# Row-tiled attention scores for two heads at once, with a 0/1 mask multiplied in on VectorE

## The chip, the cores and the metric

The kernel runs on one core of a Trainium2 chip. A core has five engines with instruction streams of their own: TensorE (PE) multiplies matrices, VectorE (DVE) and ScalarE (ACT) work element by element, GpSimd (POOL) does the same on data outside the matmul result memory PSUM, and SyncE (SP) issues DMA transfers. ACT and POOL issue transfers as well. Each engine takes its instructions in the order of the program and waits on semaphores that other engines raise. Weight loads of PE are shown apart as PEld; they run beside the matmuls. SBUF is the on-chip data memory, PSUM takes the matmul results.

The metric is the device time of one execution in microseconds; the median over the runs counts. The kernel before takes 332.96 us (three runs, 329.74 to 333.13).

## What is computed

Block-sparse attention (4 batches, 8 heads, 768 positions, head size 64), followed by a feed-forward layer with a squared relu. The mask consists of 32x32 blocks: neighbours, the first and last block row and column, and three sampled blocks per row.

```python
scores = scale * np.matmul(q, k.transpose(0, 1, 3, 2))
...
scores = np.where(mask, scores, -1000000000.0)
scores = scores - np.max(scores, axis=-1, keepdims=True)
attn = np.exp(scores)
attn = attn / (np.sum(attn, axis=-1, keepdims=True) + 1e-09)
return np.matmul(attn, v).astype(np.float32)
...
h = x @ w_in            # x: heads side by side, 3072 x 512; w_in 512 x 2048
r = np.maximum(h, 0.0)
g = r * r
return (g @ w_out).astype(np.float32)
```

## The kernel before

**Units.** Heads are taken in pairs. A pair of one batch is a unit `u` (16 of them, four per batch). The 768 queries are cut into three parts `qi` of 256, the 768 keys into six blocks of 128, taken two at a time as `cp` (three). One slot `(u, qi, cp)` is the score tile of two key blocks and two heads against 256 queries; there are 144. Batch 0 goes through its four pairs for `qi` = 0, then for 1 and 2; the later batches go unit by unit.

**A slot.** `scores` (L319) makes four matmuls of 256 columns into a PSUM tile `ps` (two buffers, L66). `exps` (L332) turns the tile into `pT` on ACT, one instruction of 128x1024 to bf16, seven buffers. `values` (L337) makes four matmuls into `po` (one buffer). `VA` and `VB` hold V of one head in one half and ones in the other, so `po` also holds the sums. After three slots `inverse` (L352) makes 1/sum with three ACT instructions (Ln, Ln, Exp), and `normalize` (L361) multiplies on DVE into `xT`.

**The mask before.** It costs no instruction of its own in a slot. Of the 128 rows that a matmul contracts over, 64 hold the head and 24 more hold the mask: in the keys a one-hot of the key's block (`oh`, L200), in the queries minus 8e9 where that block is not allowed (`bm`, `pb`, L232 to L241). So the contraction has 88 rows, and the product is already masked. The two heads lie in separate tiles `QK[i][:, which, h]`, 24 mask rows under each; they are copied there by DMA (`key_rows`, `query_rows`) or, from batch 1 on, come in through the transposing DMA from the tiles `CQ`, whose columns 64 to 87 hold the mask (`mask_columns`, L250).

**Preparing a unit.** Q, K and V of a pair are loaded as fp32 by three DMAs (`load`, L144). For batch 0, Q and K are cast on DVE, transposed on PE (`transp`, L274) and moved to `QK` on DVE, one copy per head (`evac`, L282). Later units are cast on DVE into `CQ` (`cast_t`, L287) and transposed by DMA, four per unit (`transp_dma`, L290). V is cast on POOL for the units 1 to 3 and on DVE for the others (L269).

**Feed-forward.** Nine tiles of 256 (batch 0) or 384 positions. `hidden` (L376): for each of 16 blocks of `w_in` four matmuls into `ph` (two buffers, shared with the transposes), relu on DVE (`relu`, L387), the square on POOL (`square`, L392). `output` (L400): 16 matmuls of 512 columns into `py` (one buffer), copied out by ACT (L411) and stored by SP. A tile needs all four pairs of its batch, so the feed-forward of a batch runs beside the attention of the next, and the rest at the end. The weights come through POOL's DMA queue, `w_in` first (L303).

**What sets the order.** Every step is a `Task` with an engine, an assumed duration, a priority and its dependencies (L79). `run_schedule` (L108) plays these through once at build time: the engine that can start first takes its ready task of lowest key. The order it comes to is the fixed instruction order of each engine. On the chip only the semaphores act; where a step takes longer than assumed, everything behind it on its engine waits. Attention has keys from 0 to 143 (relus 0), hidden and output from 1000 on, so PE takes attention work where it is ready, and feed-forward work otherwise.

The softmax here doesn't subtract the row's maximum and nothing guards it: scores larger than these inputs give would overflow.

## Time and profile before

One execution was taken by the hardware profiler. It took 334.34 us, of which 332.6 lie in the span of its records.

| | |
|---|---|
| median of three runs | 332.96 us |
| the profiled execution / its span | 334.34 us / 332.6 us |
| first exp / first hidden matmul | 11.5 us / 38.9 us |
| first hidden matmul of batch 1 | 140.4 us |
| last value matmul | 264.5 us |
| exp of a slot, 128x1024 (ACT, L334) | 144 of 1.017 us on average |
| the three instructions of `inverse` (ACT, L356 to L358) | 48 each, 0.381, 0.376 and 0.416 us |
| the two of `normalize` (DVE, L367, L368) | 48 each, 0.414 and 0.427 us |
| relu of 128x384 (DVE, L389), square (POOL, L395) | 96 each, 0.557 and 0.837 us |

Engines overlap, so busy times do not add up to the span. Matmuls are pipelined: the profile gives 0.27 us for one of 256 columns, but the next starts 0.109 us later. In the views that list instructions, a line has the start in us, the length, the engine, the line of the program, the operation, output <- input with their shapes, and in square brackets how long the engine had been idle and what ended that. In the grouped view a line has the count after the x, then busy us, mean ns of one, and the idle time before them with what ended it. PEclk is the share of its clock that PE was granted.

### The profile page before, as it was taken

How to read it: one execution, taken by the hardware profiler on the slowest of the kernel's cores; microseconds unless marked ns; L12 is line 12 of the kernel's file. 1: busy time of each engine (PE TensorE's matmuls, PEld its weight loads, DVE VectorE, ACT ScalarE, POOL GpSimd, SP SyncE). 2: the span in 40 equal slices, each digit the busy share in tenths (PEclk: the TensorE clock that was granted, in tenths of full speed). 3: DMA queues.
4: the chain of work that ended last, by engine and by line, in shares of the span. 5: the costliest groups of instructions: out<-in, count | busy, mean ns of one | idle time of the engine just before them, and what ended most of it. 6: DMA issues, size and time to landing. Idle time of an engine off the chain costs nothing. (4 is left out here: it accounts for less than half of the span.)

```text
span 332.6 us, 5743 instructions
## 1 busy us (share of the span) xinstructions
PE 306.5 (92%) x2174; PEld 209.8 (63%) x2174; DVE 156.6 (47%) x336; ACT 210.2 (63%) x317; POOL 129.3 (39%) x183
## 2 busy tenths in 40 slices
PE   2878899999978978999999999999999999999994
PEld 1555687777855756677776766777776655555541
DVE  7674244885454532366545334344334454444410
ACT  5479897859857778887786978888886301000011
POOL 6157143452422310055444232322223456666610
PEclk9999799999999999999999999999999999999999
DMA  7989995599999997482326200000000000100002
GB/s 228 233 195 206 199 289 211 120 250 229 216 285 239 246 271 225 95 204 42 62 67 73 55 2 32 2 32 3 32 33 1 34 33 32 63 34 32 34 32 96
DMA packets 59561, 39.61 MB, mean 119 GB/s; under 512 B 39790, under 2 KB 56462, under 8 KB 59534
## 3 DMA queue, kind: packets, MB, share of 16 engines
q1 hardware_dynamic: 55038, 34.66, 41.2%
q0 software_dynamic: 4224, 4.19, 7.8%
q10 hardware_dynamic: 272, 0.39, 0.3%
q8 instruction: 17, 0.28, 0.3%
q14 instruction: 10, 0.08, 0.1%
HBM read 27.26 MB, written 6.29 MB: 101 GB/s over the span
## 5 line engine op out<-in xcount | busy, mean ns | idle before, releaser
L395 POOL TENSOR_TENSOR g<-r 128x384 bf16<-128x384 f32 (+1 forms) x144 | 111.0, 776 | 175.7 <-DVE r L389 175.5
L334 ACT ACTIVATE pT<-ps 128x1024 bf16<-128x1024 f32 x144 | 140.9, 1017 | 41.2 <-PE po L349 32.0
L384 PE MATMUL ph<-xT,w_in_sb 128*128 128x384 bf16 (+1 forms) x576 | 120.0, 308 | 2.3 <-DVE r L389 2.1
L389 DVE TENSOR_SCALAR r<-ph 128x384 f32<-128x384 f32 (+1 forms) x144 | 73.1, 512 | 98.3 <-PE ph L384 72.8
L408 PE MATMUL py<-w_out_sb,g 128*128 128x512 bf16 x384 | 110.1, 379 | 0.8 <-ACT ys L413 0.8
L384 PEld LDWEIGHTS <-w_in_sb 128*128 128x128 bf16 x576 | 56.2, 98 | 38.2 <-issue 3.6
L347 PE MATMUL po<-pT,VA 128*128 128x256 bf16 x288 | 71.3, 274 | 7.7 <-DVE xT L368 4.6
L326 PE MATMUL ps<-QK 88*128 88x256 bf16 x288 | 72.6, 277 | 3.0 <-ACT pT L334 1.6
L328 PE MATMUL ps<-QK 88*128 88x256 bf16 x288 | 72.0, 276 | 0.4 <-DVE QK L285 0.2
L349 PE MATMUL po<-pT,VB 128*128 128x256 bf16 x288 | 71.1, 274 | 0.0
L413 ACT COPY ys<-py 128x512 f32<-128x512 f32 x24 | 13.9, 585 | 62.5 <-PE py L408 58.6
L408 PEld LDWEIGHTS <-g 128*128 128x128 bf16 x384 | 37.5, 98 | 22.0 <-issue 1.3
L347 PEld LDWEIGHTS <-VA 128*128 128x128 bf16 x288 | 28.2, 98 | 19.5 <-issue 8.6
L328 PEld LDWEIGHTS <-QK 88*128 88x128 bf16 x288 | 28.6, 99 | 10.4 <-issue 2.3
L326 PEld LDWEIGHTS <-QK 88*128 88x128 bf16 x288 | 28.2, 98 | 9.2 <-issue 1.9
L349 PEld LDWEIGHTS <-VB 128*128 128x128 bf16 x288 | 28.3, 98 | 8.7 <-issue 1.6
L367 DVE TENSOR_TENSOR xT<-po,rs 64x256 bf16<-64x256 f32 x48 | 19.9, 414 | 29.0 <-ACT rs L358 27.3
L356 ACT ACTIVATE ls<-po 64x256 f32<-64x256 f32 x48 | 18.3, 381 | 10.2 <-PE po L349 9.1
L358 ACT ACTIVATE rs<-ls 128x256 f32<-128x256 f32 x48 | 20.0, 416 | 1.5
L368 DVE TENSOR_TENSOR xT<-po,rs 64x256 bf16<-64x256 f32 x48 | 20.5, 427 | 0.6
L357 ACT ACTIVATE ls<-po 64x256 f32<-64x256 f32 x48 | 18.1, 376 | 0.6
L288 DVE CAST CQ<-ks 128x768 bf16<-128x768 f32 x12 | 6.9, 578 | 11.8 <-DMA QK<-CQ 11.7
(49 smaller groups left out, 76.2 us busy)
## 6 DMA issues: line engine op xcount, KB each, us to landing
qs<-in_q_dram SPq DMA_DIRECT2D x16, 384.0 KB, 6.2
vs<-in_v_dram SPq DMA_DIRECT2D x16, 384.0 KB, 8.1
out_dram<-ys SPq DMA_DIRECT2D x24, 256.0 KB, 2.1
ks<-in_k_dram SPq DMA_DIRECT2D x15, 384.0 KB, 8.7
w_in_sb<-in_moe_w_in_dram POOLq DMA_DIRECT2D x4, 512.0 KB, 8.2
w_out_sb<-in_moe_w_out_dram POOLq DMA_DIRECT2D x4, 512.0 KB, 13.4
QK<-CQ SPq DMA_TRANSPOSE x48, 4.0
ks<-in_k_dram ACTq DMA_DIRECT2D x1, 384.0 KB
```

Source lines behind the costliest of these rows:

```text
L326: nc.tensor.matmul(ps[:, c, 0, :], KA[i][0:64 + nb, ksl], QA[i][0:64 + nb, qsl], start=True, stop=True)
L328: nc.tensor.matmul(ps[:, c, 1, :], KB[i][0:64 + nb, ksl], QB[i][0:64 + nb, qsl], start=True, stop=True)
L334: nc.scalar.activation(out=pT, in_=stile.pop((u, qi, cp)), func=AF.Exp, scale=scale)
L347: nc.tensor.matmul(po[:, 0, :], VA[i][:, n, :], pT[:, c, 0, :], start=first, stop=last, skip_group_check=True)
L349: nc.tensor.matmul(po[:, 1, :], VB[i][:, n, :], pT[:, c, 1, :], start=False, stop=last, skip_group_check=True)
L358: nc.scalar.activation(out=rs, in_=ls, func=AF.Exp, scale=-1.0)
L367: V.tensor_mul(out=xT[b][0:D, a, qsl], in0=po[0:D, 0, :], in1=rs[0:D, :])
L368: V.tensor_mul(out=xT[b][D:P, a, qsl], in0=po[D:P, 1, :], in1=rs[D:P, :])
L384: nc.tensor.matmul(ph, w_in_sb[:, kc, f * P:(f + 1) * P], xT[b][:, kc, c0:c0 + w], start=(kc == 0), stop=(kc == KM - 1))
L389: V.tensor_scalar(out=r, in0=htile.pop((T, f)), scalar1=0.0, scalar2=None, op0=AOP.max)
L395: G.tensor_mul(out=g, in0=r, in1=r)
L408: nc.tensor.matmul(py, gtile[T, f][:, ts * P:(ts + 1) * P], w_out_sb[:, f, :], start=(f == 0), stop=(f == NF - 1))
```

## The change

**Row tiling.** Q and K of a pair now lie in one tile each, `QT` and `KT`, head 0 in the rows 0 to 63 and head 1 in the rows 64 to 127. A score matmul contracts over 64 rows; the matmuls of the two heads are issued in turn and go to different rows of the array, and their results to different PSUM banks (`ps[:, h, c]`). The planner takes the slots one by one in the batches 0 and 1 (72 slots) and from batch 2 on two at a time, eight matmuls in a row.

**The mask.** It becomes a 0/1 tile of bf16, `mask`, made once by 18 matmuls over 24 rows (`mask_product`) and nine DVE copies (`mask_copy`). After the exp of a slot, `mask_mul` multiplies `pT` by it in place, on DVE for 138 slots and on POOL for six (slots 14, 18, 22, 26, 30 and 34); `values` waits for that.

**Preparation.** The mask rows, their copies and `CQ` go. Units of batch 0 load Q in three parts, the first pair also K in two; their casts go to POOL, apart from K and the first part of Q of the first pair, which stay on DVE; each part has its transposes and one copy out. Later units are cast on DVE and transposed by two DMAs. All V casts go to POOL. There are nine `pT` buffers instead of seven, and the `w_out` loads come with the first unit of batch 1 instead of right after `w_in`.

**Relu.** From batch 1 on, every third block (`f % 3 == 2`, five of 16) has its relu on ACT: 30 in all.

```diff
-    def load(u, eng):
+    def load(u):
         b, a = divmod(u, HP)
-        qs = ld.tile([P, 2, NCH, D], F32, name="qs", tag="qs")
-        ks = ld.tile([P, 2, NCH, D], F32, name="ks", tag="ks")
-        vs = ld.tile([P, 2, NCH, D], F32, name="vs", tag="vs")
-        nc.sync.dma_start(out=qs.rearrange("p t n d -> p t (n d)"), in_=qv[b, a])
-        eng.dma_start(out=ks.rearrange("p t n d -> p t (n d)"), in_=kv[b, a])
-        nc.sync.dma_start(out=vs.rearrange("p t n d -> p t (n d)"), in_=vv[b, a])
-        raw[u] = (qs, ks, vs)
...
+    def load_part(eng, u, w, c0, c1):
+
+        if u not in raw:
+            raw[u] = [None, None, None]
+        if raw[u][w] is None:
+            name = ("qs", "ks", "vs")[w]
+            raw[u][w] = ld.tile([P, 2, NCH, D], F32, name=name, tag=name, bufs=NRAW + (w == 0))
+        b, a = divmod(u, HP)
+        cols = slice(c0 * 2 * D, c1 * 2 * D)
+        eng.dma_start(out=raw[u][w].rearrange("p t n d -> p t (n d)")[:, :, cols],
+                      in_=(qv, kv, vv)[w][b, a][:, :, cols])
+
+    load_part(nc.scalar, 0, 1, 0, 1)
+    load_part(nc.sync, 0, 0, 0, 1)
     sb_i = consts.tile([nb, n_rand * 2], I32, name="sb_i")
-    nc.sync.dma_start(out=sb_i, in_=sampled_blocks.bitcast(I32))
-    load(0, nc.scalar)
-    load(1, nc.sync)
+    nc.scalar.dma_start(out=sb_i, in_=sampled_blocks.bitcast(I32))
+    load_part(nc.sync, 0, 1, 1, CP)
+    load_part(nc.sync, 0, 2, 0, CP)
+    load_part(nc.sync, 1, 1, 0, CP)
+    load_part(nc.sync, 1, 0, 0, 1)
+    load_part(nc.sync, 1, 2, 0, CP)
...
-    def key_rows(i):
-        nc.sync.dma_start(out=QK[i][MR, 1], in_=oh[:, None, :].broadcast_to([nb, 2, S]))
-
-    for h in range(2):
-        nc.scalar.copy(out=QK[0][MR, 1, h, :], in_=oh)
...
-    bm = consts.tile([nb, MR.stop], BF, name="bm")
-    V.memset(bm, 0.0)
-    V.tensor_scalar(out=bm[:, MR], in0=pm[:, cur, :], scalar1=-1.0, scalar2=-NEG,
-                    op0=AOP.add, op1=AOP.mult)
-
-    pb = ps_s.tile([P, 1024], F32, name="pb", tag="ps")
...
-    def mask_columns(w):
-        pc = ps_h.tile([P, S], BF, name="pc", tag="h")
-        src = KA[0] if w else QA[0]
...
+    def rows_product():
+        pb = ps_s.tile([P, 1024], F32, name="pb", tag="ps")
+        nc.tensor.matmul(pb[0:nb, 0:512], bm, oh[:, 0:512], start=True, stop=True)
+        nc.tensor.matmul(pb[0:nb, 512:S], bm, oh[:, 512:S], start=True, stop=True)
+        mtile["rows"] = pb
+
+    def rows_copy():
+        nc.scalar.copy(out=bq, in_=mtile.pop("rows")[0:nb, 0:S])
...
+    def mask_product(qi, cp):
+        pq = ps_y.tile([P, 2, QW], F32, name="pq", tag="y")
+        for c in range(2):
+            n = cp * 2 + c
+            nc.tensor.matmul(pq[:, c, :], oh[:, n * P:(n + 1) * P], bq[:, qi * QW:(qi + 1) * QW],
+                             start=True, stop=True)
+        mtile[qi, cp] = pq
+
+    def mask_copy(qi, cp):
+        V.tensor_copy(out=mask[:, qi, cp * 2:cp * 2 + 2, :], in_=mtile.pop((qi, cp)))
...
+    def cast_qk(eng, u, w, c0, c1):
+
+        c = work.tile([P, NCH, 2, D], BF, name="qc", tag="qc", bufs=QC_BUFS)
+        ns = slice(c0 * 2, c1 * 2)
+        eng.tensor_copy(out=c[:, ns], in_=raw[u][w][:, :, ns, :].rearrange("p t n d -> p n t d"))
+        cast[u, w, c0] = c
...
-        (G if 0 < u < HP else V).tensor_copy(out=dst, in_=vs[:, h])
-
...
+    def evac(u, w, c0, c1):
+        dst = (KT if w else QT)[u % NPB]
+        cols = slice(c0 * 2 * P, c1 * 2 * P)
+        V.tensor_copy(out=dst[:, cols], in_=ptp.pop((u, w, c0))[:, cols])
 
     def transp_dma(u, w):
-        for h in range(2):
-            dst = QK[u % NPB][:, w, h, :]
-            nc.sync.dma_start(out=dst.rearrange("r (n p) -> r n p", p=P),
-                              in_=CQ[w][u % NCQ][:, h].rearrange("p n r -> p (n r)"), transpose=True)
+        dst = (KT if w else QT)[u % NPB]
+        nc.sync.dma_start(out=dst.rearrange("r (n p) -> r n p", p=P),
+                          in_=cast.pop((u, w, 0)).rearrange("p n t d -> p (n t d)"), transpose=True)
...
-    def scores(u, qi, cp):
-        i = u % NPB
-        ps = ps_s.tile([P, 2, 2, QW], F32, name="ps", tag="ps")
-        qsl = slice(qi * QW, (qi + 1) * QW)
-        for c in range(2):
-            n = cp * 2 + c
-            ksl = slice(n * P, (n + 1) * P)
-            nc.tensor.matmul(ps[:, c, 0, :], KA[i][0:64 + nb, ksl], QA[i][0:64 + nb, qsl],
-                             start=True, stop=True)
-            nc.tensor.matmul(ps[:, c, 1, :], KB[i][0:64 + nb, ksl], QB[i][0:64 + nb, qsl],
-                             start=True, stop=True)
-        stile[u, qi, cp] = ps
+    def scores(slots):
+        for u, qi, cp in slots:
+            i = u % NPB
+            ps = ps_s.tile([P, 2, 2, QW], F32, name="ps", tag="ps")
+            qsl = slice(qi * QW, (qi + 1) * QW)
+            for c in range(2):
+                n = cp * 2 + c
+                for h in range(2):
+                    nc.tensor.matmul(ps[:, h, c, :], KT[i][h * D:(h + 1) * D, n * P:(n + 1) * P],
+                                     QT[i][h * D:(h + 1) * D, qsl], start=True, stop=True)
+            stile[u, qi, cp] = ps
...
+    def mask_mul(eng, u, qi, cp):
+        pT = ptile[u, qi, cp]
+        eng.tensor_mul(out=pT, in0=pT,
+                       in1=mask[:, None, qi, cp * 2:cp * 2 + 2, :].broadcast_to([P, 2, 2, QW]))
...
+    def relu_eng(T, f):
+        return "ACT" if T[0] and f % 3 == 2 else "DVE"
...
-    PT_BUFS, R_BUFS, G_BUFS = 7, 4, 2 * NF + 3
+    PT_BUFS, R_BUFS, G_BUFS, QC_BUFS = 9, 4, 2 * NF + 3, 5
...
+    for qi in range(NQ):
+        for cp in range(CP):
+            s = qi * HP * CP + cp - (4 if qi else -0.4)
+            t = Task("PE", 0.4, s, (lambda a=(qi, cp): mask_product(*a)), deps=[rc],
+                     get="y", **pe)
+            mk[qi, cp] = Task("DVE", 0.62, s, (lambda a=(qi, cp): mask_copy(*a)), deps=[t], put=[t], **SEM)
...
+            on = "POOL" if (u or c0) and not (w and u == 0) else "DVE"
+            c = Task(on, 0.06 + (0.17 if on == "DVE" else 0.36) * n, s - 6,
+                     (lambda a=a, e=G if on == "POOL" else V: cast_qk(e, *a)), get="qc", after=at, **SEM)
+            t = Task("PE", 0.25 * n, s - 5 - w, (lambda a=a: transp(*a)), deps=[c], get="h", put=[c], **pe)
+            e = Task("DVE", 0.06 + 0.17 * n, s - 5, (lambda a=a: evac(*a)), deps=[t], put=[t], **SEM)
...
+        if u == HP:
+            for i in range(NWP, 2 * NWP):
+                wl[i] = Task("POOL", 1.0, s0 - 12 + i, (lambda i=i: w_load(i)), deps=cv[u], late=2.0, dma=8.0)
...
+    N_ONE = 72
+
+    def attend(s, slots):
+        sc = Task("PE", 0.42 if len(slots) == 1 else 0.645, s, (lambda: scores(slots)),
+                  deps=[ev[u][1, cp] for u, qi, cp in slots] + [ev[u][0, qi] for u, qi, cp in slots] + sc_all[-1:],
+                  get="ps", n=len(slots), **pe)
         sc_all.append(sc)
-        va_all.append(va)
-        sc_of[u].append(sc)
-        va_of[u].append(va)
-        if cp == CP - 1:
-            inv = Task("ACT", 1.2, s - 9, (lambda: inverse(u, qi)), deps=[va], **SEM)
-            mu[u, qi] = Task("DVE", 0.87, s - 9, (lambda: normalize(u, qi)), deps=[inv],
-                             put=[va_all[-CP]], **SEM)
+        for j, a in enumerate(slots):
+            u, qi, cp = a
+            k = s + j
+            ex = Task("ACT", 0.97, k, (lambda a=a: exps(*a)), deps=[sc], get="pT", put=[sc.bufs[j]], **SEM)
+            pool = 12 <= k < 36 and k % 4 == 2
+            mm = Task("POOL" if pool else "DVE", 2.3 if pool else 0.7, k - 1,
+                      (lambda a=a, e=G if pool else V: mask_mul(e, *a)), deps=[ex, mk[qi, cp]], **SEM)
+            va = Task("PE", 0.44, k + 2.2, (lambda a=a: values(*a)), deps=[mm] + cv[u] + va_all[-1:],
```

## The prediction

> **What bounds the kernel now.** I read the page's busy shares and slices first, then the busy times cut at the places where the program changes character, then single instructions.
>
> ```profile
> PE 306.5 (92%) x2174; PEld 209.8 (63%) x2174; DVE 156.6 (47%) x336; ACT 210.2 (63%) x317; POOL 129.3 (39%) x183
> ...
> PE   2878899999978978999999999999999999999994
> ```
>
> TensorE (PE) is nearly always busy, but its busy time counts pipelined matmuls, so I price it by start-to-start distances. Four stages: until the first hidden-layer matmul (38.9 us), until the first one of batch 1 (140.4), until the last value product (264.5), and the rest.
>
> ```profile
> 39.00:140.00 101.00, 93.15 (x742) 71.39 (x740) 53.97 (x124) 80.18 (x122) 31.66 (x50) 1.00 0.93 224
> 140.00:264.00 124.00, 123.93 (x905) 87.50 (x904) 56.06 (x114) 96.43 (x147) 46.45 (x55) 1.00 0.20 47
> 264.00:333.00 69.00, 63.57 (x334) 32.43 (x332) 23.26 (x43) 7.52 (x14) 33.61 (x41) 0.99 0.12 43
> ```
>
> The columns after the length are PE, weight loads, DVE, ACT, POOL. In the third stage PE has no free time, while DVE has 68 us and ACT 28 us. Matmuls there start 0.109 us apart at 256 columns, 0.161 at 384, 0.216 at 512 (timeline: 19 of the last take 4.26 us). In that stage: 266 score and 296 value matmuls at 0.109, 224 hidden at 0.161, 120 output at 0.216 make 61.3 + 36.1 + 25.9 = 123 of 124 us. So a microsecond taken from PE there is a microsecond off the end. In the second stage the same count gives 91 of 101 us; the first is bound by its chain of small steps.
>
> **The scores on PE.** Before, 576 matmuls at 0.109 us are 62.8 us. After, two heads sit in 64-row halves; if they run side by side, 288 steps make 31.4. Changing between 64-row, 32-row and 128-row use costs something. The trace shows one such change, around the 24-row transposes of L254:
>
> ```profile
> 31.21 0.27 PE L347 MATMUL po<-pT,VA 128*128 128x256 bf16 x1
> 31.32 0.27 PE L349 MATMUL po<-pT,VB 128*128 128x256 bf16 x1
> 31.53 0.31 PE L254 MATMUL pc<-identb,QK 24*128 24x24 bf16 x6
> 31.77 0.28 PE L326 MATMUL ps<-QK 88*128 88x256 bf16 x1
> 31.89 0.27 PE L328 MATMUL ps<-QK 88*128 88x256 bf16 x1
> ```
>
> Going in, the start is 0.21 us after the previous one instead of 0.109: 0.10 lost. The six are 0.028 apart ((0.31 - 0.168)/5), so the last starts at 31.67, and the next full matmul 0.10 later: 0.07 lost. A round trip is 0.17; I take 0.18. In the program after, the scores form 104 groups (64 of one slot, 40 of two). A two-slot group costs 0.436 + 0.18 = 0.62 us against 0.874, a one-slot group 0.40 against 0.437. So 40 x 0.257 + 64 x 0.039 = 12.8 us saved. Nine mask products add 18 x 0.109 = 2.0 us and about four more round trips, 0.7; L254's transposes take 0.5 away. Net -10.6 us.
>
> No row shows two matmuls side by side. Bounds: overlap complete, -10.6; none, 31.4 more, +20.8. I take complete overlap: the halves read separate rows and the two heads write separate banks (`ps[:, h, c]`), and the six transposes at 0.028 us show that weights load far faster than one per 0.109.
>
> The Trainium skill speaks against that: "TensorE: Matmul & The Clock Gate", Part 3, measures 3.07x for four 32-row tiles, 77% of ideal. If two halves reached that too, a pair would take 0.142 us (an estimate from that page) and the change would save about 9.5 us less.
>
> **By stages on PE.** I cut the program after at the same landmarks. Second stage: 228 score matmuls in 57 groups, 114 x 0.109 + 57 x 0.18 = 22.7; 224 values 24.4; 192 hidden at 0.109, 20.9; 88 outputs 19.0: 87.0 against 91. Third: 264 scores in 33 groups, 14.4 + 5.9; 296 values 32.3; 259 hidden 41.7; 154 outputs 33.3: 127.6. Fourth: 124 hidden and 142 outputs remain instead of 160 and 170, 11.6 us less. Third and fourth together: +3.6 - 11.6 = -8 us, with 0.6 for the few records missing in the trace: -8.6.
>
> **The mask on DVE.** 138 multiplies of 128x1024 bf16 (six more on POOL), nine mask copies, all between exp and values. The nearest rows:
>
> ```profile
> L285 DVE COPY QK<-pt 64x768 bf16<-64x768 bf16 x16 | 8.7, 553 | 1.5 <-PE pt L278 1.1
> L258 DVE COPY CQ<-pc 128x144 bf16<-128x144 bf16 x8 | 1.4, 226 | 2.7 <-PE pc L254 2.6
> L389 DVE TENSOR_SCALAR r<-ph 128x384 f32<-128x384 f32 x96 | 53.5, 557 | 75.9 <-PE ph L384 52.7 <-POOL g L395 20.1 <-PE po L349 2.0
> L389 DVE TENSOR_SCALAR r<-ph 128x256 f32<-128x256 f32 x48 | 19.6, 421 | 22.4 <-PE ph L384 20.1 <-PE po L349 1.7
> ```
>
> Pure bf16 grows by 327 ns per 624 elements, giving 687 ns at 1024; fp32 by 136 ns per 128, giving 1237. L367, with two inputs, goes the slow way (414 ns at 256), but in fp32 from PSUM. I take 0.69, because all three operands are bf16; 1.24 stays as the upper end.
>
> It may also wait for POOL. A cast did, behind a square:
>
> ```profile
> 142.37 1.00 POOL L395 TENSOR_TENSOR g<-r 128x384 bf16<-128x384 f32 x1 [22.46 <-DVE r L389]
> 142.60 0.98 DVE L272 CAST VB<-vs 128x384 bf16<-128x384 f32 x1
> ```
>
> That cast takes 0.35 alone. The 26 V casts on DVE average 0.48, so 0.13 per instruction is lost; I charge it to each multiply (bounds 0, as most casts were not held, and 0.63, as here). These casts read one SBUF operand; no row has two. The Trainium skill, "SBUF — State Buffer", section "Who interferes with whom", says a DVE instruction with two SBUF inputs does contend with a POOL instruction that reads SBUF; by it the charge holds, without it DVE would have 18 us less.
>
> Third stage on DVE: 72 x (0.69 + 0.13) = 59, 25 normalizations at 0.84 = 21, 14 casts at 0.56 = 8, 45 relus at 0.557 = 25: 113 of 128 us. ACT: 72 exps at 0.975, 25 inversions at 1.18, some 20 moved relus near 0.49 (between L358's 0.42 and L413's 0.585), ten copies: 115. So PE still ends last, but both engines that feed it rise from 45% and 78% to about 90%. Behind each multiply on DVE stand relus, and PE waits for those through two hidden buffers; a two-slot group also needs both score buffers empty at once. I charge 4 us of new PE stalls (bounds 0, and 12.6 if PE falls to the 90% it shows in the second stage).
>
> Second stage: PE 87 plus the 9.7 idle now is 97; DVE: 51 multiplies (42), normalizations 16, relus 20, casts 6, total 84. I take 98, 3 less than now.
>
> **The start.** K and Q of the first pair arrive in parts, but the first cast meets POOL's eight memsets as it does now:
>
> ```profile
> 4.63 2.76 DVE L266 CAST qc<-ks 128x768 bf16<-128x768 f32 x1
> ```
>
> It needs 0.55 alone and ended at 7.39, after the last memset (6.97). The memsets stay where they are, so the first cast again ends near 7.1, and the first exp comes near 9.2 instead of 11.5. Then DVE carries, until the fourth pair's first normalization: 16 multiplies 11.0, nine mask copies at about 0.69, 6.2, evacuations 5.2 (15 of 0.28 to 0.55), normalizations 3.4, casts 1.1, lock waits 2.1: 29 us from 7.1, hence 36, against 34.5 now. Earlier data is taken up by the mask. I book the first hidden matmul at 38, 0.9 us sooner. Cover that hides the rest: SP issues 20 part loads instead of 11 loads and six row copies, all before its wait for the weights; POOL's Q and K casts and six multiplies (1.76 each by L395's slope, 653 to 837 ns per 128) fill idle POOL time (48% busy there at most). If POOL ran late, w_in would arrive later than its present 27 to 34 us. The output weights now load after the 15th square and are first used after the 23rd hidden tile; at some 2 us per tile (48 in 101 us) that is 16 us against a median landing of 13.4, so the cover is thin. The DMA transposes drop from 48 to 24 and the 16.8 us that DVE waits for CQ buffers go; DVE has idle time there, so I book nothing.
>
> **Sum.** -0.9 - 3 - 8.6 + 4 = -8.5 us on the profiled execution (334.34 us, span 332.6 and 1.7 around it), so 325.8. The runs' median, 332.96, lies 1.4 below that execution: **324.5 us**.
>
> **Rivals.**
> 1. Everything keeps up: no stalls in stage three, and the start gains 5 us. -8.5 - 4 - 4 = 316. For it: 10% slack on ACT and DVE. Against: DVE's 29 us at the start.
> 2. Gain cancelled: PE falls to 90% in stage three, 12.6 us of stalls: 333. For it: ACT already waits 17 us there for value products, and two-slot groups tie both buffers. Against: nine exp buffers instead of seven.
> 3. Slower: DVE becomes the bound in stage three. Other DVE work is 54 us, so from (127.6 - 54)/72 = 1.02 us per multiply, waits included, DVE ends last. At 1.24: stage three +11, stage two +7, start +9: 352; the middle of this case is 343. For it: L367's rate, POOL waits of 0.63. Against: L285.
> 4. The halves do not overlap: +31.4 us on PE, some 28 where PE ends last: 352. Against it only the layout.
>
> **Chances.** Forecast (319 to 330) 0.45, rival 1 0.13, rival 2 0.17, rival 3 0.15, rival 4 0.10. The range 313 to 346 leaves out most of rival 4, the upper end of 3 and the lowest of 1. This kernel's measurement tells about 1% from no change, 329.6 to 336.3. Faster: 0.42 of the forecast's, rival 1 and 0.03 of rival 2: 0.58. Same: 0.03 and 0.10: 0.13. Slower: the rest, 0.29.
>
> **What would show it.** Score pairs starting 0.11 us apart and groups of 0.62 us; multiplies of 0.69 with some near 1.2; first hidden matmul near 38, first of batch 1 near 136, last value product near 267. Score matmuls at 0.109 each mean rival 4; multiplies over 1.02 rival 3; long ACT waits for scores rival 2. What would upset all of it is a data wait that the present loads hide, in w_out above all.

## The result and the profile after

The changed kernel takes **342.21 us** (median of four runs, 341.63 to 344.24) against 333.04 beside it: 1.031 times the time before, 95% interval 1.023 to 1.039. The forecast was 324.5; its range holds the result, its sign is wrong. The profiled execution took 341.63 us, its span 339.9.

The page of the kernel after, busy shares and slices:

```profile
PE 305.2 (90%) x2180; PEld 169.3 (50%) x2180; DVE 238.5 (70%) x414; ACT 221.2 (65%) x344; POOL 187.1 (55%) x225
...
PE   3978787739899999999999999999999998999994
...
PEclk9998997976999999999999999999999999999999
```

The last slices look as before. The hole is in the third to tenth slice, 17 to 85 us, and the granted clock dips there too. The stages, cut at the same landmarks (columns as in the prediction: PE, PEld, DVE, ACT, POOL, granted clock, DMA share, GB/s):

```profile
37.25:150.00 112.75, 96.93 (x735) 53.62 (x733) 89.59 (x152) 79.58 (x120) 58.51 (x71) 0.94 0.45 114
150.00:283.75 133.75, 130.57 (x975) 76.31 (x973) 104.18 (x173) 104.51 (x169) 76.66 (x76) 1.00 0.28 84
283.75:340.00 56.25, 51.45 (x268) 25.89 (x265) 12.96 (x24) 11.24 (x22) 26.22 (x32) 1.00 0.11 43
```

| stage | before | forecast | after |
|---|---|---|---|
| 1, to the first hidden matmul | 38.9 | 38 | 37.3 |
| 2, to the first one of batch 1 | 101.5 | 98 | 112.6 |
| 3, to the last value product | 124.1 | 131.6 | 133.8 |
| 4, the rest | 68.1 | 56.4 | 56.3 |

One stage misses, the second, by 14.6 us. PE's longest waits in it (what waits, for whom: total us, times, longest us), first in the kernel before, then in the one after:

```profile
PE po L347 <- DVE xT L368: 4.1, 4, 1.7
PE ph L384 <- DVE r L389: 2.1, 1, 2.1
```
```profile
PE ph L399 <- DVE r L410: 8.0, 8, 1.9
PE ps L338 <- DMA QT<-qc: 5.7, 1, 5.7
PE po L362 <- DVE xT L383: 1.1, 5, 0.3
```

So hidden matmuls wait longer for relus on DVE (`r`), 8.0 us in place of 2.1, there is one new wait of 5.7 us for a transposed Q, and value matmuls wait less for normalizations (`xT`). Busy time hides gaps between pipelined matmuls, so I went through all start-to-start distances on PE. From each I took what the matmul needs (0.109, 0.161, 0.216 us by columns, half of 0.109 for a score matmul that shares the array) and, at a change into or out of the tiling, up to 0.105. What remains is time lost, to waits or to a lower clock. The distances start at the first matmul and end at the last.

| us | needed | changes | lost in stage 1 | 2 | 3 | 4 | span |
|---|---|---|---|---|---|---|---|
| before | 289.9 | 0 | 17.2 | 10.1 | 1.2 | 1.5 | 332.6 |
| after | 260.1 | 21.1 | 13.7 | 25.1 | 5.5 | 1.4 | 339.9 |
| w_out early | 260.1 | 21.2 | 14.4 | 14.6 | 7.9 | 1.4 | 335.7 |
| w_out later | 260.1 | 21.2 | 15.0 | 17.2 | 3.1 | 1.7 | 334.1 |
| no multiplies, planned anew | 260.1 | 21.7 | 13.0 | 9.0 | 2.9 | 1.4 | 321.1 |
| last version | 260.1 | 20.4 | 18.8 | 9.9 | 5.2 | 1.3 | 329.3 |

The rows below the second are experiments. Each row is one profiled execution, which can lie some us from the median (w_out early: 337.80 profiled, 335.48 in the median). Between the first two: 29.8 less needed, 21.1 for changes, so PE's own work falls by 8.7 us; 15.7 more are lost, 15.0 of them in stage 2. Together +7.0, of 7.3 us that the span grew.

The row tiling does what it says. Timeline of the kernel after, PE:

```profile
199.92 0.27 PE L364 MATMUL po<-pT,VB 128*128 128x256 bf16 x1
200.12 0.61 PE L338 MATMUL ps<-QT,KT 64*128 64x256 bf16 x8
200.67 0.28 PE L362 MATMUL po<-pT,VA 128*128 128x256 bf16 x1
```

From 199.92 to 200.67 are one value matmul and the eight scores of a two-slot group: 0.75 - 0.109 = 0.64 us; 0.62 was forecast. Less the changes, 0.44 remain for eight, four steps of 0.109: the two halves overlap fully. The 3.07x that the Trainium skill, "TensorE: Matmul & The Clock Gate", Part 3, gives for four 32-row tiles is 77% of four; such a loss is not seen here with two tiles.

The multiplies, in the groups of the kernel after (count, busy us, mean ns, idle before and its cause):

```profile
L349 DVE TENSOR_TENSOR pT<-pT,mask 128x1024 bf16<-128x1024 bf16 x138 | 115.9, 855 | 25.7 <-ACT pT L344 23.8
L416 POOL TENSOR_TENSOR g<-r 128x384 bf16<-128x384 f32 x96 | 94.2, 989 | 79.2 <-DVE r L410 66.1 <-ACT r L408 12.8
L349 POOL TENSOR_TENSOR pT<-pT,mask 128x1024 bf16<-128x1024 bf16 x6 | 14.2, 2372 | 5.6 <-ACT pT L344 5.6
```

The shortest multiply on DVE takes 674 ns, the median 693, the longest 2461. The six on POOL take 2372 ns on average. The squares on POOL grew from 837 to 989 ns. Each engine holds the other up; in a timeline (start, length) around one multiply on POOL:

```profile
41.96 2.57 POOL L349 TENSOR_TENSOR pT<-pT,mask 128x1024 bf16<-128x1024 bf16 x1
...
43.08 3.02 DVE L349 TENSOR_TENSOR pT<-pT,mask 128x1024 bf16<-128x1024 bf16 x2 [0.53 <-ACT pT L344]
...
46.02 0.41 DVE L410 TENSOR_SCALAR r<-ph 128x256 f32<-128x256 f32 x1
```

Two multiplies, 1.4 us by themselves, took 3.02 beside it and the square behind it (44.49 to 45.54), and the relu behind them, for which PE waits, stood until 46.02.

Then the largest single stall. Timeline of the kernel after:

```profile
62.92 2.29 POOL L321 DMA_DIRECT2D w_out_sb<-in_moe_w_out_dram  x3
...
63.42 1.31 SPq L304 DMA_TRANSPOSE KT<-qc  x1
...
64.83 1.78 SPq L304 DMA_TRANSPOSE QT<-qc  x1
```
```profile
76.58 1.03 PE L338 MATMUL ps<-QT,KT 64*128 64x256 bf16 x8 [5.68 <-DMA QT<-qc]
...
77.73 0.42 PE L364 MATMUL po<-pT,VB 128*128 128x256 bf16 x1
77.95 0.42 PE L362 MATMUL po<-pT,VA 128*128 128x256 bf16 x1
78.16 0.42 PE L364 MATMUL po<-pT,VB 128*128 128x256 bf16 x1
```

The w_out loads, now issued with the first unit of batch 1, begin 0.5 us ahead of that unit's K transpose and 1.9 us ahead of its Q transpose; three of the four are issued before Q's. Q then lands 11.7 us after its issue, where the median of the twelve is 2.5, and PE stands for 5.7 us. Afterwards it runs at half speed: values start 0.215 apart in place of 0.109, until about 81.9. The work from 76.58 to 81.84 needs 3.0 us and took 5.3, so the stall costs some 8 us, not 5.7. The Trainium skill, "TensorE: Matmul & The Clock Gate", Part 1, says that the clock halves after an idle window of about 3.4 us and comes back after about as much sustained work; behind this stall the trace agrees in kind and shows 5.3 us of half speed.

The stall is not the only place with a halved clock. Windows of the kernel after (the third number from the end is the granted clock):

```profile
54.00:58.00 4.00, 4.00 (x23) 2.51 (x22) 2.17 (x6) 2.05 (x2) 3.44 (x4) 0.57 0.02 4
66.00:70.00 4.00, 2.86 (x17) 1.99 (x17) 3.66 (x6) 0.00 (x0) 4.00 (x3) 0.78 1.25 192
78.00:82.00 4.00, 4.00 (x23) 1.87 (x22) 2.13 (x4) 2.68 (x5) 0.99 (x1) 0.52 1.10 289
82.00:86.00 4.00, 4.00 (x35) 2.14 (x34) 3.33 (x8) 3.52 (x5) 2.45 (x4) 1.00 0.02 4
```

The clock is halved from 54.6 to 58.0, from 68.2 to 71.6 and from 75.0 to 81.9 us. In the kernel before it was full through the whole second stage (the prediction's row has 1.00). The first two stretches stand behind waits for relus of 1.8 and 1.9 us, which ended at 53.22 and 66.99. Those waits are shorter than the page's idle window, so on this point the measurement differs from the page. Not every wait of that length does it: in the second stage before, one of 2.1 us did not. By the distances the two stretches cost some 2.8 us.

### The profile page after: what moved, and what is told of

The parts are those of the page before. It is cut to its first block, busy times and chain, and to the rows that moved or that the text cites. A ratio compares the mean times of both kernels' runs of the same rounds, so it can differ in the third digit from the quotient of the medians.

```text
span 339.9 us, 5897 instructions
## 1 busy us (share of the span) xinstructions
PE 305.2 (90%) x2180; PEld 169.3 (50%) x2180; DVE 238.5 (70%) x414; ACT 221.2 (65%) x344; POOL 187.1 (55%) x225
## 5 line engine op out<-in xcount | busy, mean ns | idle before, releaser
L416 POOL TENSOR_TENSOR g<-r 128x384 bf16<-128x384 f32 (+1 forms) x144 | 131.4, 922 | 125.9 <-DVE r L410 108.5
L349 DVE TENSOR_TENSOR pT<-pT,mask 128x1024 bf16<-128x1024 bf16 x138 | 115.9, 855 | 25.7 <-ACT pT L344 23.8
L399 PE MATMUL ph<-xT,w_in_sb 128*128 128x384 bf16 (+1 forms) x576 | 117.9, 310 | 8.5 <-DVE r L410 8.5
L410 DVE TENSOR_SCALAR r<-ph 128x384 f32<-128x384 f32 (+1 forms) x114 | 55.9, 499 | 45.2 <-PE ph L399 31.7
L362 PE MATMUL po<-pT,VA 128*128 128x256 bf16 x288 | 75.4, 286 | 4.1 <-DVE xT L383 2.4
L364 PE MATMUL po<-pT,VB 128*128 128x256 bf16 x288 | 75.1, 286 | 0.0
L338 PE MATMUL ps<-QT,KT 64*128 64x256 bf16 x576 | 51.8, 281 | 9.0 <-DMA QT<-qc 5.7
L338 PEld LDWEIGHTS <-KT 64*128 64x128 bf16 x576 | 20.5, 95 | 36.9 <-issue 31.6
L408 ACT ACTIVATE r<-ph 128x384 f32<-128x384 f32 x30 | 14.6, 488 | 28.1 <-POOL g L416 19.7
L371 ACT ACTIVATE ls<-po 64x256 f32<-64x256 f32 x48 | 18.2, 380 | 15.6 <-PE po L364 14.7
L382 DVE TENSOR_TENSOR xT<-po,rs 64x256 bf16<-64x256 f32 x48 | 19.7, 409 | 10.7 <-ACT rs L373 10.0
L434 ACT COPY ys<-py 128x512 f32<-128x512 f32 x24 | 13.9, 582 | 17.3 <-PE py L429 13.6
L349 POOL TENSOR_TENSOR pT<-pT,mask 128x1024 bf16<-128x1024 bf16 x6 | 14.2, 2372 | 5.6 <-ACT pT L344 5.6
## 6 DMA issues: line engine op xcount, KB each, us to landing
w_out_sb<-in_moe_w_out_dram POOLq DMA_DIRECT2D x4, 512.0 KB, 10.9
```

The costliest lines, as they stand in the source:

```text
L338: nc.tensor.matmul(ps[:, h, c, :], KT[i][h * D:(h + 1) * D, n * P:(n + 1) * P], QT[i][h * D:(h + 1) * D, qsl], start=True, stop=True)
L349: eng.tensor_mul(out=pT, in0=pT, in1=mask[:, None, qi, cp * 2:cp * 2 + 2, :].broadcast_to([P, 2, 2, QW]))
L362: nc.tensor.matmul(po[:, 0, :], VA[i][:, n, :], pT[:, 0, c, :], start=first, stop=last, skip_group_check=True)
L364: nc.tensor.matmul(po[:, 1, :], VB[i][:, n, :], pT[:, 1, c, :], start=False, stop=last, skip_group_check=True)
L382: V.tensor_mul(out=xT[b][0:D, a, qsl], in0=po[0:D, 0, :], in1=rs[0:D, :])
L399: nc.tensor.matmul(ph, w_in_sb[:, kc, f * P:(f + 1) * P], xT[b][:, kc, c0:c0 + w], start=(kc == 0), stop=(kc == KM - 1))
```

## Experiments

The theory after this reading: stage 2 pays for the multiplies (load and mutual holding of DVE and POOL) and for the collision of w_out with the transposes. Rivals: the multiplies on POOL alone; the collision alone; the order of the work, which a plan with too short durations wrote.

Each group of runs had the kernel before measured beside it, with medians from 331.06 to 333.35 us. The differences below are those of the medians; taken from the ratios they move by up to 1.5 us.

### Which part of the change costs

**All multiplies on DVE** (the planner orders anew).

```diff
-            pool = 12 <= k < 36 and k % 4 == 2
+            pool = False
```

> All 144 mask multiplies on DVE, none on POOL; nothing else is edited, the planner orders anew. The loss against the forecast lies in the second stage (first hidden matmul to the first one of batch 1: 112.6 us where 98 were forecast). Theory A: the six multiplies on POOL, 2.1 to 2.7 us each, hold DVE's multiplies (two of DVE took 3.0 to 3.5 us beside them) and so PE. Then the second stage falls to about 104 us and the time from 342 to 334. Theory B (the w_out loads delay the transposes of the first unit of batch 1) and theory C (the order on DVE puts that unit's casts too late): the wait of 5.7 us for QT near 71 us stays, the time stays at 340 to 343, or grows by up to 5, since DVE gets six multiplies more.

340.73 us (ratio 1.025, 1.017 to 1.033), 1.5 us less by the medians, within the noise. But the second stage of this profile took 105.9 us, not 112.6, near the 104 of theory A, and PE waited less for relus there:

```profile
PE ps L338 <- DMA QT<-qc: 5.4, 1, 5.4
PE ph L399 <- DVE r L410: 3.5, 8, 1.1
```

The first stage took 40.1 us in place of 37.3 (its start was held, see below), the third 136.9 in place of 133.8. So the six multiplies on POOL do cost time in the second stage; how much of it they cost at the end, this run does not tell. The wait for Q stays.

**Scores without row tiling** (contracting over all 128 rows, which sums the two heads).

```diff
-    nc.tensor.matmul(ps[:, h, c, :], KT[i][h * D:(h + 1) * D, n * P:(n + 1) * P],
-                     QT[i][h * D:(h + 1) * D, qsl], start=True, stop=True)
+    nc.tensor.matmul(ps[:, h, c, :], KT[i][:, n * P:(n + 1) * P],
+                     QT[i][:, qsl], start=True, stop=True)
```

> The score matmuls contract over all 128 rows, so no row tiling in the scores and no change of tiling around them; the heads are not kept apart (each result is the sum of both heads), which leaves the number, the sizes and the order of all instructions as they are. It gives the time that row tiling itself is worth. If the gain on PE reaches the end: 10 us of PE more, of which the third stage (no idle PE) carries 8: 342 to 350 or 352. If the tiled scores are hidden behind ACT and DVE: 342 to 344.

348.21 us (1.049, 1.041 to 1.057). The tiling brings 6.0 us at the end, of some 12 on PE (291.5 needed here and 2.0 for changes around the mask products, against 260.1 + 21.1).

**No multiplies** (the masked keys stay in), order planned anew.

```diff
-            mm = Task("POOL" if pool else "DVE", 2.3 if pool else 0.7, k - 1, ...)
-            va = Task("PE", 0.44, k + 2.2, ..., deps=[mm] + cv[u] + va_all[-1:], ...)
+            va = Task("PE", 0.44, k + 2.2, ..., deps=[ex] + cv[u] + va_all[-1:], ...)
```

> The mask is still built but not multiplied in, on no engine; the values follow the exps directly, and the planner orders anew. It gives the price of all multiplies together. If they are the whole loss (theory A and the load on DVE): second stage near 95 us, no stalls in the third, 342 to about 322. If the loss of the second stage comes from the late start of batch 1 (theories B and C): the wait for QT stays, about 330.

323.25 us (0.974, 0.967 to 0.981): 19.0 us less, and the squares are back at 861 ns:

```profile
L416 POOL TENSOR_TENSOR g<-r 128x384 bf16<-128x384 f32 x96 | 82.0, 861 | 96.4 <-DVE r L410 78.1 <-ACT r L408 18.2
```

Here the w_out loads went out 0.2 us behind the Q transpose (58.51 and 58.30), Q landed in 4.7 us and did not hold PE up. So the 19 us are not the multiplies alone.

**Multiplies left out in batch 0 alone (`k < 36`), order kept.**

```diff
-  (lambda a=a, e=G if pool else V: mask_mul(e, *a)), ...
+  (lambda a=a, e=G if pool else V, skip=k < 36: None if skip else mask_mul(e, *a)), ...
```

> The instruction order is that of the changed kernel; only the 36 multiplies of batch 0 are left out, so the values of batch 0 are summed over unmasked weights. In the trace of the changed kernel, multiply 8 starts 1.6 us later than the order's own plan has it, multiply 20 8 us, multiply 28 22 us, and the last one still 22 us: the time is lost between 22 and 79 us. Theory A (VectorE's load in that stretch, multiplies beside GpSimd's and the batch-0 preparation, makes the delay, and the wait for the transposed Q behind the w_out loads adds some 6 us): 342 falls to 326 to 331. Rival B (each multiply costs about the same wherever it is, 36 of 144 of 19 us): 337.

337.68 us (1.016, 1.009 to 1.022).

The same from batch 1 on (`k >= 36`), those of batch 0 done:

> Same order, and the 108 multiplies from batch 1 on are left out, those of batch 0 done. Theory A: the delay is there already when batch 1's multiplies begin, so 342 falls by 2 to 5 only, to 337 to 340. Rival B (108 of 144 of 19 us): 328.

339.01 us (1.023, 1.018 to 1.027). My theory A expected 326 to 331 for the first and falls there, but its 337 to 340 for the second was right; B's 337 was right for the first, its 328 for the second was not. The two savings, 4.5 and 3.2, do not make 19. The trace without the multiplies of batch 0 shows why:

```profile
69.20 1.04 PE L338 MATMUL ps<-QT,KT 64*128 64x256 bf16 x8 [7.78 <-DMA QT<-qc]
```

Its loads went out at 55.86, again ahead of the transposes (56.66, 58.08). Batch 0 is done earlier, and PE only waits longer for Q, which lands in 11.1 us here. In the second run Q takes 11.1 us too.

### The collision

**w_out early**, right behind w_in, as in the kernel before.

```diff
-            for i in range(NWP):
+            for i in range(2 * NWP):
                 wl[i] = Task("POOL", 1.0, first[u] + i, ...)
...
-        if u == HP:
-            for i in range(NWP, 2 * NWP):
-                wl[i] = Task("POOL", 1.0, s0 - 12 + i, ...)
```

> The w_out loads are issued right after the w_in loads, as in the kernel before, in a stretch (34 to 55 us) in which the DMA engines now stand still. Theory B: the transposes of unit 4 no longer share the DMA engines with 4 MB of weights, land in 2.5 us instead of 11.7, PE's wait of 5.7 us for QT goes and what stands behind it: 342 to about 335. Theory C: the casts of unit 4 still start near 62 us, so its scores start near 69 instead of 76.6; 342 to 338. Theory A: 341 to 343.

335.48 us (1.011, 1.007 to 1.014): 6.7 us less.

**w_out later**, behind the transposes.

```diff
-    (lambda i=i: w_load(i)), deps=cv[u], late=2.0, dma=8.0)
+    (lambda i=i: w_load(i)), deps=cv[u], after=62.0, late=2.0, dma=8.0)
```

> The changed kernel with one thing moved: the four w_out loads stand about 5 us later in GpSimd's order, so that the transposes of unit 4 are issued ahead of them. In the changed kernel the first load was issued 0.5 us ahead of the first transpose and Q came 11.7 us after its issue; in the kernel without multiplies 1.6 us behind it, and Q came in 4.7. If the order of issue decides: Q lands in about 5 us, and 342 falls by 5 to 7, to 335 to 337. If sharing the transfer engines is enough whatever the order: 340 to 343.

335.38 us (1.012, 1.005 to 1.019): 6.8 us less from the other side. Timeline and, below it, the Q tile between 60 and 80 us of this kernel:

```profile
66.58 1.30 SPq L304 DMA_TRANSPOSE KT<-qc  x1
67.99 1.23 SPq L304 DMA_TRANSPOSE QT<-qc  x1
73.22 2.29 POOL L321 DMA_DIRECT2D w_out_sb<-in_moe_w_out_dram  x3
```
```profile
DMA to landing us min/median/max: 2.6/2.6/2.6
```

Q lands in 2.6 us. The loads go out 10.3 us later than before and 2.7 us after Q has landed, so this run parts the two in time. That the order of issue decides where they do overlap is seen across the runs. With the first load 1.0 us ahead of the Q transpose, as in the runs with all multiplies on DVE, without row tiling and with one slot everywhere, Q took 10.9 to 11.2 us. With it 0.2 us behind, in the run without multiplies, Q took 4.7. Stage 2 loses 17.2 us in place of 25.1. Of these 7.9 us, 5.4 are the wait for Q; the clock is full here from 43 to 143 us, so the half speed goes with it, in the two other places too. The waits for relus stay (8.5 us).

**No multiplies with w_out early, order kept** (weights unmasked).

```diff
-  (lambda a=a, e=G if pool else V: mask_mul(e, *a)), ...
+  (lambda a=a, e=G if pool else V, skip=True: None if skip else mask_mul(e, *a)), ...
```

> The kernel with early w_out loads, in its own order, without any mask multiply (the weights stay unmasked). It tells what the multiplies cost where no transfer collides. If the multiplies by their own time make the other part of the loss: 335.5 falls by 10 to 13, to 322 to 326, near the 323 of the kernel without multiplies whose order was planned anew. If most of their 19 us came from the collision, or from the new planning: 331 to 334.

325.72 us (0.981, 0.971 to 0.990). With no collision in the way all multiplies together cost 9.8 us, half of the 19.

### The start

In the kernels after, the first exp came at 8.1 us in some profiles and at 10.7 to 11.4 in others, with the same instructions ahead of it. Timelines of the kernel after and of the one with later w_out loads:

```profile
3.93 0.16 DVE L242 CAST sbf<-sb_i 24x3 f32<-24x3 int32 x1 [1.11 <-DMA sb_i<-in_sampled_blocks_dram]
4.02 0.43 POOL L203 MEMSET VA<- 128x384 bf16 x1
```
```profile
4.02 0.42 POOL L203 MEMSET VA<- 128x384 bf16 x1
4.08 2.89 DVE L242 CAST sbf<-sb_i 24x3 f32<-24x3 int32 x1 [1.26 <-DMA sb_i<-in_sampled_blocks_dram]
...
6.53 0.42 POOL L204 MEMSET VB<- 128x384 bf16 x1
```

A cast of 24x3 elements that starts 0.09 us before the first of eight memsets takes 0.16 us; one that starts 0.06 after it is held until the last one ends. In the profile of the kernel after the start was not held, so the hold has no part in its 341.63 us. Whether it was held in the executions without a profile is not known; it makes up to 3 us, so a difference of that size between medians of four runs can come from it.

**Memsets apart**, on the kernel with later w_out loads (the plan also lets POOL start at 4.9 us, not 7.5).

```diff
-    for i in range(HP):
-        init_v(G, i)
+    init_v(G, 0)
...
+        early = [Task("POOL", 0.8, first[u] - 3, (lambda u=u: init_v(G, u)), after=land_v[u] - 1.0, **SEM)] if u else []
```

> The kernel with later w_out loads (335.4), and only the two memsets of the first pair at the start on GpSimd; the other six stand between its casts later. In the profiles the small cast of the sampled blocks on VectorE took 0.16 us where it started at 3.93, before the first of eight memsets (4.02), and 2.9 to 3.0 where it started at 3.96 or 4.08, until the last memset ended; the first exp came at 8.1 and at 10.7 to 11.4. If that hold costs what it delays: first exp near 8.1 in every run, 335.4 falls by 2 to 3, to 332.5 to 333.5. If the start is taken up again by the mask and the batch-0 work on VectorE: 335, within 1 us.

332.55 us (1.003, 0.999 to 1.006): 2.8 us less. Behind two memsets the cast took 0.78, and the first exp came at 8.55.

### Pairs, plan and relus

**One slot per change everywhere.**

```diff
-    N_ONE = 72
+    N_ONE = 144
```

> The changed kernel with one slot per tiling change everywhere: 36 more groups. By the trace a change into and out of the tiling costs 0.21 us, so 7.5 us more on TensorE in the last two stages. If the two-slot groups cause no stalls, 349. If the idle time that the third stage gained (5 us against the kernel before) comes from waiting until both score buffers are empty, it goes and the time is near 344.

349.37 us (1.057, 1.053 to 1.061), the value for "no stalls": 36 more groups cost 7.2 us by the medians (8.7 by the ratios), 0.20 to 0.24 each; in the trace the changes take 7.3 us more, 0.20 each. Stage 3 loses some 5.5 us as before. The pairs of batch 2 and 3 cause no stalls.

**w_out early, planned with 3.0 us per weight load.**

```diff
-                             dma=8.0 if i < 2 else 5.2)
+                             dma=3.0)
```

> The w_out loads follow w_in again, and the plan assumes 3.0 us for a weight load instead of 8.0 and 5.2, near what the trace shows, so the loads, casts and transposes of unit 4 stand some 14 us earlier in the order. If the late place of unit 4 costs something beside the collision with w_out, this gives 330 to 333; if the collision was all, it stays at 335.5, the time with w_out early alone.

334.13 us (1.010, 1.006 to 1.013): 1.4 less than without, within what the measurement tells.

**The same with pairs from batch 1 on** (`N_ONE = 36`).

> w_out early, the plan with 3.0 us per weight load, and two slots per tiling change already in batch 1: 18 changes fewer at 0.20 us (36 more of them cost 7.2 us in the run with one slot everywhere). If TensorE's time ends last in batch 1 too: 334.1 falls by 3 to 4, to 330 to 331. If batch 1 is held up by VectorE and ScalarE, so that the pairs only wait longer: 334 to 336.

338.83 us (1.020, 1.010 to 1.030), slower than either expectation. Windows of the kernel with single slots in batch 1, then of this one:

```profile
120.00:140.00 20.00, 14.72 (x116) 7.22 (x114) 13.78 (x25) 17.27 (x29) 1.22 (x3) 1.00 0.51 126
```
```profile
120.00:140.00 20.00, 14.10 (x92) 7.03 (x89) 11.85 (x20) 14.71 (x24) 2.83 (x4) 0.74 0.43 139
```

There the hidden matmuls of batch 0 are used up and PE has only attention and some output matmuls left. Single slots keep ACT busy for 17.3 of 20 us, pairs for 14.7: a pair waits until both score buffers are empty, so scores and exps take turns, and from 120 to 146 us ACT waited 5.5 us for scores where it had waited 1.6. The granted clock is 0.74 in place of 1.00 in these windows, halved from 127.7 us on, in a wait of 2.9 us. Changes cost 3.6 us less, as expected, but stage 2 loses 20.0 us where it lost 12.7; some 4 of these 7.3 us are the halved clock. In batch 2 and 3 feed-forward work fills that wait.

**Pairs, and the durations of the trace in the plan.**

```diff
-            ex = Task("ACT", 0.97, k, ...)
+            ex = Task("ACT", 1.02, k, ...)
-            mm = Task(..., 2.3 if pool else 0.7, k - 1, ...)
+            mm = Task(..., 2.3 if pool else 0.83, k - 1, ...)
-    SQ = {256: (0.44, 0.44, 0.62), 384: (0.652, 0.57, 0.88),}
+    SQ = {256: (0.44, 0.44, 0.79), 384: (0.652, 0.57, 0.99),}
```

> As the run with pairs from batch 1 on, and the plan has the durations of the trace: multiply 0.83 for 0.70, exp 1.02 for 0.97, squares 0.79 and 0.99 for 0.62 and 0.88, casts 0.80 for 0.60. If stalls come from an order made for a faster VectorE and GpSimd, 2 to 4 us less than with the old durations, 326 to 329; if the engines' load itself makes them, the same time within 1 us.

334.12 us (1.008, 1.003 to 1.013): 4.7 less, but not the 326 to 329 expected.

**A third of batch 0's relus on ACT**, with later w_out loads.

```diff
-        return "ACT" if T[0] and f % 3 == 2 else "DVE"
+        return "ACT" if f % 3 == 2 else "DVE"
```

> The kernel with later w_out loads (335.4), and every third relu of batch 0 on ScalarE too (15 of 48). In the second stage TensorE's longest waits are now for relus on VectorE (8.5 us, 8 times), while VectorE is busy for 9 of 10 us and ScalarE for 6 to 8. If VectorE's load is what is left of the loss: the second stage gains 4 to 6 us and the time is 330 to 332. If the waits only move to another step (exps behind relus on ScalarE): 334 to 337.

339.70 us (1.021, 1.013 to 1.029), 4.3 more. Waits of PE from 35 to 145 us in this kernel (total, times, longest):

```profile
PE ph L399 <- DVE r L410: 5.8, 12, 1.2
PE po L362 <- ACT pT L344: 3.4, 3, 1.8
PE ps L338 <- DMA QT<-qc: 2.1, 1, 2.1
PE po L362 <- DVE xT L383: 2.0, 5, 0.8
```

With the relus on DVE the first was 8.5 us, the others 1.8, 0.3 and 0.6 (from 40 to 143 us): the waits move to exps, normalizations and Q.

**Both**, memsets and relus:

> Both edits on the kernel with later w_out loads. If both causes hold and add up: 327 to 330. If only the start holds: 332.5 to 333.5; only the relus: 330 to 332; neither: 335.

336.37 us (1.015, 1.006 to 1.023). The memsets take 3.3 us off here too; the relus still cost, 3.8 us against the run with the memsets alone.

**Both, with w_out early:**

> Both edits, with the w_out loads right behind w_in in place of later (335.5 with early loads alone). The same sums: 327 to 330 if both hold. It tells whether the place of the loads matters once they do not collide with the transposes: within 2 us of the run before it if not.

332.14 us (1.004, 1.001 to 1.008), 4.2 less than with the loads later, so the place does matter; which transfer or wait makes that difference was not followed up.

**What can be had back.** w_out early, 3.0 us per weight load, the measured durations (a cast at 0.80), single slots up to batch 1, memsets apart:

> w_out early, 3.0 us per weight load in the plan, the plan with the durations of the trace, single slots in batches 0 and 1, and the memsets apart. If the parts add up: 334.1 (w_out early, planned anew) less 2.8 (memsets) and less up to 4.7 (what the measured durations gave the run with pairs from batch 1 on), 327 to 331.5. If the plan's durations only mended the pairs: 331 to 332, the time of the kernel before.

333.99 us (1.006, 1.002 to 1.010): the parts do not add up. The same with all multiplies on DVE:

> As the run before it, with all 144 multiplies on VectorE. On the changed kernel alone that took 1.5 us off. If multiplies on GpSimd hold VectorE longer than six multiplies cost it: 1 to 2 us less than the run before it. If VectorE's load in batch 0 is the limit: 2 to 4 us more.

**330.73 us** against 331.26 for the kernel before, ratio 0.997 (0.995 to 1.000): level with it, 3.3 less than the version before it. With the other edits in, multiplies on POOL do hold DVE up by more than six multiplies cost. In the profile of this version the needed work and the changes come to 280.5 us, 9.4 less than in that of the kernel before, and 35.2 us are lost in place of 30.0; the rest is lost ahead of the first matmul or behind the last. (That profile of the kernel before, 334.34 us, lies 3 us above its median of this round.)

## Why the prediction was wrong

**PE's own work: right.** The net -10.6 us came out as -8.7. (One product in the sum of the stages is 0.2 us off: 36 hidden and 28 output matmuls are 11.8 us, not 11.6.) A two-slot group was given 0.62 us and takes 0.64; the round trip is 0.20 us, not 0.18, over 104 groups that is the difference. Stage 2 was to need 87.0 us on PE; needed and changes there make 76.8 + 10.8 = 87.6.

**The multiplies: priced right.** 0.69 + 0.13 = 0.82 us were charged, 0.855 measured; DVE in stage 2 was given 84 us and had 89.6. The charge for mutual holding, for which the Trainium skill, "SBUF — State Buffer", section "Who interferes with whom", spoke, is borne out on both engines. Only those on POOL were priced too low: 1.76 us each from the slope of the squares, 2.37 measured, and what they hold up on DVE was not in the sum.

**The step that failed:** "PE 87 plus the 9.7 idle now is 97; [...] I take 98". The time lost in stage 2 was carried over from the kernel before as a constant. It went from 10.1 to 25.1. Two things were left out:

- Some 8 us are the collision, 5.7 of stall and 2.3 of half clock behind it. The moved w_out loads were followed to their own consumer only ("16 us against a median landing of 13.4, so the cover is thin"). That cover held: no wait of PE for w_out is in the trace. Late was the Q transpose of the first unit of batch 1, issued 1.9 us behind the first of them. The forecast's warning of a data wait "in w_out above all" named the transfer and not its victim. Moving the loads either way took 6.7 and 6.8 us off.
- Some 7 us follow the multiplies' load in a stage where PE waits for what DVE and POOL do. The waits for relus rose from 2.1 to 8.0 us, and the half clock behind two of them cost some 2.8; waits for normalizations fell from 4.1 to 1.1. DVE's sum, 84 of 98 us, was set down as fitting. But the batch-0 relus stand behind a held multiply, and the two hidden buffers did not bridge it. With the loads later, stage 2 loses 17.2 us and waits 8.5 for relus; without multiplies, 9.0 and 1.0. With all multiplies on DVE it waits 3.5, so those on POOL have a share in it.

**The start** was sized for one case of two. First exp "near 9.2": 8.1 or about 11. The forecast held the eight memsets against the first cast of K; in the changed order a smaller cast stands ahead of it and meets them or not by a tenth of a microsecond. Parting them is worth 2.8 us on the kernel with later loads, whose profile had a held start. The profile of the kernel after did not: its first exp came at 8.1 and its first stage was 0.7 us shorter than forecast.

**Stages 3 and 4: right.** 4 us of new stalls were charged; stage 3 lost 4.3 more. The stages took 133.8 and 56.3 us, against 131.6 and 56.4.

**The rivals.** Rival 3's 343 us is near the result by chance: it put DVE over PE in stage 3, from 1.02 us per multiply on. Rival 4 is excluded by the groups of 0.64 us. Rival 2 put 12.6 us of stalls into stage 3, which lost 4.3 us more; the larger stalls came in stage 2.

By the profiled executions the miss is 15.8 us, 341.63 against 325.8: 14.6 in stage 2, 2.2 in stage 3, and 0.8 gained in the other two, to within the rounding. The other 2 us are the step to the medians: 1.4 was taken off, and the median came out 0.6 above the profiled execution. By the experiments the collision is worth 6.7 or 6.8 us, and all multiplies cost 9.8 without it, of which 4 had been charged as stalls in stage 3. How far these sums overlap stays open: the runs differ by 1%, some edits did not add up, and half clock comes with some waits and not with others.

## What to carry to other kernels

When a large transfer is moved, list every transfer that is issued near its new place, on any queue, and ask who waits for those; that its own consumer comes late enough says nothing about them. Idle time of an engine in a stage is not a constant to carry into a forecast: here DVE's busy share of the second stage rose from 53% to 79%, and short holds on it became PE's waits. Work taken off the bounding engine at the price of work on its feeders paid here only in the last two stages (190.1 us in place of 192.2), where another kind of work fills the gaps.

## What the hardware showed

- A transposing DMA that lands in 2.5 us by the median took 10.9 to 11.7 when the first of four loads of 512 KB was issued 1.0 to 2.2 us ahead of it (six kernels), 4.7 when it was issued 0.2 us behind it, and 2.6 when it was issued 5.2 us behind it.
- A stall of 5.7 us on PE cost another 2.3, since it ran at half clock for 5.3 us. Waits of 1.8 and 1.9 us were each followed by 3.4 us of half clock as well, another of 2.1 us was not.
- A 24x3 cast on DVE that began 0.06 us behind the first of eight back-to-back POOL memsets took 2.89 us in place of 0.16; with only two memsets, 0.78.
- Two bf16 multiplies on DVE took 3.02 us beside a multiply and a square on POOL, in place of 1.4, and POOL's 128x384 squares went from 861 to 989 ns when multiplies ran on DVE.
